# Dummy matmuls in TensorE's idle time, later assumed DMA landings, and expert squares kept in PSUM by VectorE

## The chip, the cores and the metric

One core of a Trainium2 chip runs the whole program. The metric is device time in microseconds, from the start of the launch to its end, lower is better. Engines are named as in the profile: PE is TensorE (PEld its weight loads), DVE is VectorE, ACT is ScalarE, POOL is GpSimd, SP is the engine whose queue issues nearly all DMAs.

## What is computed

Three blocks follow each other: a linear attention with product features, an expert block (two matrix products with a squared ReLU between them and a sigmoid gate), and a gated block that mixes along the sequence with a 1088 x 1088 matrix.

```python
# attention, per batch b and head h (4 x 4, 1088 positions, head width 32, r = 8)
phi(x) = outer(S1 x, S2 x)                    # 64 features
out = phi(q) (phi(k)^T v) / (phi(q) . sum phi(k) + 1e-6)
# expert block, x is (4, 1088, 128)
xk, xr = mu_k*x + (1-mu_k)*x_prev, mu_r*x + (1-mu_r)*x_prev
k = max(xk @ w_k, 0)                          # 128 -> 1024
x = sigmoid(xr @ w_r) * (k*k @ w_v)           # 1024 -> 128
# gated block
h = max(x @ w_in, 0); u, v = halves of h      # 128 -> 2 x 512
v = layernorm(v) over its 512 columns
v_s = w_spatial @ v + b_spatial               # along the 1088 positions
out = (u * v_s) @ w_out                       # 512 -> 128
```

## The kernel before

Everything is kept transposed, features on the 128 partitions and positions along the free axis, and a batch is cut into three chunks of 384, 384 and 320 positions (`CH`). A product that needs full accuracy is made of three passes (`mm3`): each operand is split into a high part H and a low part L of type fp32r, and L·H, H·H and H·L are added up in one PSUM bank.

**Start (0 to 30 us of the trace).** SP loads k, q, v and the expert weights. The weights come as 64-bit numbers and are taken apart by DVE, ACT and POOL (`split64`, L399 to L419). Meanwhile PE makes the attention features of batch 0 (L468, small 64 x 64 products), sums k features over positions (`k_sum`), turns q features (L549) and so on; DVE spreads features into products (L497) and masks the sums (L527). Two groups of matmuls on a zero tile do no work for the result: seven at L1135 and three at L1200, both 384 columns wide into PSUM bank 7.

**Expert loop (30 to about 170 us).** There are 96 units g: 4 batches x 3 chunks x 8 slices of 128 hidden columns. `up(g)` is an `mm3` into one of the PSUM banks 0, 1 and 2, taken in turn, and a ReLU by ACT (L655). `sqsplit(g)` squares and splits. `down(g)` adds the unit's part into bank 3. In the written order a unit's down stands four units behind its up (`LAG`). The letter that `kind(g)` takes from `PAT` says how the square is made:

- P: ACT writes r = ReLU; POOL makes r·r in SBUF (L658); ACT makes H by a second activation (Square, L687); DVE makes L = square - H from SBUF (L395). The bank is free after the ReLU.
- Q: DVE multiplies the bank by r into SBUF (L663); ACT copies that to H; POOL subtracts to L (L395). The bank is free after DVE's multiplication.
- D: ACT squares r once (L675); the down product then runs in plain fp32 (L699, two passes on PE). The bank is free after the ReLU.

Before, `PAT` gives Q to the 13 even units below 26 and P to the 30 even units from 26 to 84 and to 86, 88, 90, 92 and 94; the odd units are D, but for 87, 89, 91 and 93, which are Q.

**Spatial part (from about 150 us).** The w_spatial tiles are loaded into the two small tiles `st`, converted to H and L (`wconv`), and used by `spatial` for batch 0, then by `group` for batches 1 to 3, where sums of quadrants (`sums`, DVE at L914, from raw tiles that `wraw` loads at L911) save products.

**What sets the order.** The program is written in one order, and `arrange` at the end makes another of it: it plays all instructions through with assumed costs (`cost`), gives every engine the ready instruction of lowest rank (written place), assumes when each DMA lands, and then fixes the order on each engine, SP's queue included. So a changed instruction or a changed assumption moves others.

Of the kernel before, what the change touches and what calls it, by code (L numbers as in the profile page):

```python
# [30 lines left out]
VS = (34, 40, 43, 49, 55, 60, 63, 66, 69)  # L31
VN = (72, 85)
CONVP = (512,)
NWARM = 7
NFILL = 3
NFILL2 = 3
VP = 2 * (HD + 1)
G1 = 26
WS = 30
# [14 lines left out]
EP = 2  # L54
G2 = (86, 94)
V2 = 3
PAT = ('QD', 'PD', 'PQ', 'PD')
UT = 'x0'
GLB = 8
GW = 4  # L60
# [29 lines left out]
START = 700  # L90
LEAD = 130
MODE = {64: 93, 128: 100}
SLACK = {"PE": 60, "Activation": 150, "DVE": 150, "Pool": 200, "SP": 0}
RATES = ((3500, 200), (6400, 125), (float("inf"), 352))

# [130 lines left out]
    return type(i).__name__ == "InstDMACopy"  # L226


def arrange(tc, after, chain):

# [31 lines left out]
    for k in reversed(range(len(todo))):  # L264
        if k in follow:
            rank[k] = min(rank[k], rank[follow[k]])

    def release(k):
        e = eng[k]
# [8 lines left out]
    while left:  # L278
        pick = None
        for e in ENGINES:  # L280
            if e == "PE" and forced is not None:
                if forced not in open_[e]:
                    continue
                c = (max(free[e], ready[forced]), forced)
            else:
                if e not in best:
                    first = min((max(free[e], ready[k]) for k in open_[e]), default=None)
                    best[e] = None if first is None else min(
                        (rank[k], k, max(free[e], ready[k])) for k in open_[e] if ready[k] <= first + SLACK[e])
                if best[e] is None:  # L290
                    continue
                c = best[e][2], best[e][1]
            if pick is None or c < pick:
                pick = c
        s, k = pick
        e, i = eng[k], todo[k]
        if is_dma(i):
            if len(lanes) >= 8:
                s = max(s, done[lanes[-8]] + LATENCY[e])
            lanes.append(k)  # L300
            free[e] = s + (473 if e == "SP" else 430)
            t, size = max(s + 1080, wire), 4 * free_size(aps(i.outs)[0]) * aps(i.outs)[0].ap[0][1]
            for until, rate in RATES:
                if t < until:
                    x = min(size, (until - t) * rate)
                    t, size = t + x / rate, size - x
                    if size <= 0:
                        break
            wire = t
            done[k] = t + 450  # L310
        else:
            if e == "PE":
                if i.tile_size[1] != mode:
                    mode = i.tile_size[1]
                    s = max(s, free[e]) + MODE[mode]
                forced = follow.get(k)
            step, end, lock = spent[k]
            if lock:
                lo, hi = port["Pool" if e == "DVE" else "DVE"]
                x = hi - s - LEAD if lo <= s + LEAD < hi else 0  # L320
                step, end = step + x, end + x
                port[e] = s + LEAD + x, s + end
            free[e] = s + step
            done[k] = s + end + 10
        issued[k] = s
        order[e].append(k)
        open_[e].discard(k)
        best.pop(e, None)
        left -= 1
        for k2 in then[k]:  # L330
            missing[k2] -= 1
            if not missing[k2]:
                release(k2)
                best.pop(eng[k2], None)
# [8 lines left out]
def attn_moe_gmlp(ctx: ExitStack, tc: tile.TileContext, qT, kT, va, st, wk, wv, wr, win, wout,  # L343
# [122 lines left out]
    def tiled(out_ap, l, r, start, stop):  # L466
# [4 lines left out]
        if open_visit[0]:  # L471
            visit_last[0] = ins
        return ins

    def visit(*steps):
        open_visit[0], visit_last[0] = True, None
# [170 lines left out]
    def up(g):  # L647
# [8 lines left out]
        if kind(g) == "P":  # L656
            sq = sb(rot(*R), [128, n])
            anchor[2] = GE.tensor_tensor(out=sq, in0=r, in1=r, op=ALU.mult)  # L658
            sqs[g] = (r, sq)
        elif kind(g) == "D":  # L660
            sqs[g] = (r, None)
        else:
            anchor[0] = VE.tensor_tensor(out=r, in0=hk, in1=r, op=ALU.mult)  # L663
            sqs[g] = (None, r)

    def kind(g):
        p = PAT[(g >= G1) + sum(g >= x for x in G2)]
# [460 lines left out]
    winH, winL = sb("winH", [128, DFF], F32R), sb("winL", [128, DFF], F32R)  # L1128
    woH, woL = sb("woH", [128, DG], F32R), sb("woL", [128, DG], F32R)
    T2s = [sb(f"T2{d}", [128, 128], F32R) for d in range(ND)]  # L1130
    zero = sb("mx", [128, CMAX], F32R)
    VE.memset(zero.bitcast(F32), 0.0)
    wp = bank(7)[:, :CMAX]
    for n in range(NWARM):
        TE.matmul(wp, lhsT=zero[:, :128], rhs=zero, start=n == 0, stop=n == NWARM - 1)  # L1135
    VE.memset(ebias, -896.0 * 2 ** 23)
    VE.memset(half, -0.5)
    SE.activation(out=warm, in_=half, func=AF.Sigmoid)
# [49 lines left out]
    def behind(anchors, fn, *a):  # L1188
        fn(*a)

    def warm_up():
        wm = bank(7)[:, :CMAX]
        for n in range(NFILL2):
            TE.matmul(wm, lhsT=wkH[:, :128], rhs=wkH[:, :CMAX], start=n == 0, stop=n == NFILL2 - 1)

    now(q_feat(0, bank(4)[:, :192]))
    q_last = outer[0]
    wq = bank(7)[:, :CMAX]
    for n in range(NFILL):
        TE.matmul(wq, lhsT=zero[:, :128], rhs=zero, start=n == 0, stop=n == NFILL - 1)  # L1200
    kv0 = bank(5)
    k_sum(0, range(2), kv0, range(3))
    q_turn(0)
    k_sum(0, range(2), kv0, range(3, NT))
    k_blocks(0, kv0)
    k_mask0 = list(k_mask)
# [192 lines left out]
                    v_tile(b + 1, NK, (3, 7))  # L1399
    while gout:  # L1400
        gout.pop(0)()
    arrange(tc, after, chain)


_INS = ["qT", "kT", "va", "st", "wk", "wv", "wr", "win", "wout", "wT", "wtail", "btail", "mu", "ident", "msk"]
# [53 lines left out]
```

## Time and profile before

| | us |
|---|---|
| three runs | 446.53, 446.63, 447.45 (median 446.63) |
| profiled execution, its own time | 448.08 |
| its span from first to last instruction | 446.3 |

| engine | busy us | share |
|---|---|---|
| PE | 431.2 | 97% |
| PEld | 401.5 | 90% |
| DVE | 306.4 | 69% |
| ACT | 268.9 | 60% |
| POOL | 230.0 | 52% |

The profiled execution took 448.08 us, of which the profile's span is 446.3; the rest lies before its first and behind its last instruction. Matmul ends are modelled, so PE counts as busy even where its next matmul waits a little; the idle time of PEld and the rows of waits tell more. The mean over the span hides three stages: DVE, ACT and PE are all nearly full in the expert loop, while from 252 us on PE alone is.

### The profile page before, as it was taken

How to read it: one execution, taken by the hardware profiler on the slowest of the kernel's cores; microseconds unless marked ns; L12 is line 12 of the kernel's file. 1: busy time of each engine (PE TensorE's matmuls, PEld its weight loads, DVE VectorE, ACT ScalarE, POOL GpSimd, SP SyncE). 2: the span in 40 equal slices, each digit the busy share in tenths (PEclk: the TensorE clock that was granted, in tenths of full speed). 3: DMA queues.
4: the chain of work that ended last, by engine and by line, in shares of the span. 5: the costliest groups of instructions: out<-in, count | busy, mean ns of one | idle time of the engine just before them, and what ended most of it. 6: DMA issues, size and time to landing. Idle time of an engine off the chain costs nothing.

```text
span 446.3 us, 8451 instructions
## 1 busy us (share of the span) xinstructions
PE 431.2 (97%) x3117; PEld 401.5 (90%) x3117; DVE 306.4 (69%) x531; ACT 268.9 (60%) x629; POOL 230.0 (52%) x271
## 2 busy tenths in 40 slices
PE   8699989999999999999999899999999999999996
PEld 6587879888888889989999799999999999999996
DVE  4879989889998866576557986951847932634414
ACT  2568999989998998664344745444534434434231
POOL 2137688877886779740222646544436626334220
PEclk9569999999999999999999999999999999999999
DMA  7964020011101101421247213232022232100001
GB/s 218 365 230 146 1 56 15 20 37 47 53 20 54 35 20 36 138 61 59 104 150 217 65 61 115 84 94 64 24 84 90 78 95 62 50 10 25 2 0 50
DMA packets 31241, 34.97 MB, mean 78 GB/s; under 512 B 2848, under 2 KB 26848, under 8 KB 31200
## 3 DMA queue, kind: packets, MB, share of 16 engines
q1 hardware_dynamic: 30912, 34.36, 24.2%
q8 instruction: 24, 0.39, 0.3%
q14 instruction: 17, 0.14, 0.1%
q10 hardware_dynamic: 288, 0.08, 0.1%
HBM read 25.91 MB, written 8.52 MB: 77 GB/s over the span
## 4 chain that ended last, share of the span: by engine, by line
PE 75%; DVE 8%; ACT 6%; DMA 5%; POOL 2%; issue 1%; SPq 1%; POOLq 0%; ACTq 0%; DVEq 0%
PE p L389 61%; PE p L468 5%; PE p L699 4%; DMA m<-in_wT_dram 2%; DMA st<-in_wT_dram 2%; DMA w<-in_wk_dram 1%; ACT m L655 1%; PE p L1015 1%; PE p L1014 1%; DVE VR L797 1%; ACT w L392 1%; PE p L549 1%; DVE m L914 1%; DVE m L395 1%; ACT w L675 1%
## 5 line engine op out<-in xcount | busy, mean ns | idle before, releaser
L389 PE MATMUL p<-m,k 128*128 128x384 f32 (+1 forms) x288 | 72.4, 366 | 1.4 <-DVE m L663 1.3
L389 PE MATMUL p<-w,k 128*128 128x384 f32 (+1 forms) x360 | 63.5, 324 | 0.0
L389 PEld LDWEIGHTS p<-w,k 128*128 128x128 f32 x360 | 58.8, 188 | 0.9 <-DVE m L914 0.3
L389 PEld LDWEIGHTS p<-m,k 128*128 128x128 f32 x288 | 50.9, 194 | 9.1 <-DVE m L663 1.8
L914 DVE TENSOR_TENSOR m<-p,m 128x384 f32<-128x384 f32 (+2 forms) x37 | 19.2, 520 | 56.9 <-PE p L1015 56.4
L392 ACT ACTIVATE m<-m 128x384 fp32r<-128x384 f32 (+2 forms) x49 | 24.7, 504 | 44.6 <-DVE m L1028 35.7
L395 POOL TENSOR_TENSOR k<-VR,k 128x512 fp32r<-128x512 f32 x25 | 32.8, 1311 | 30.6 <-ACT k L392 26.1
L655 ACT ACTIVATE m<-p 128x384 f32<-128x384 f32 (+1 forms) x96 | 44.2, 470 | 7.0 <-PE p L389 5.2
L395 DVE TENSOR_TENSOR m<-m,m 128x384 fp32r<-128x384 f32 (+1 forms) x48 | 34.7, 726 | 12.3 <-ACT m L392 9.2
L389 PE MATMUL p<-w,n1H 128*128 128x384 f32 (+1 forms) x192 | 37.2, 325 | 1.0 <-DVE x L863 1.0
L658 POOL TENSOR_TENSOR m<-m 128x384 f32<-128x384 f32 (+1 forms) x35 | 30.9, 886 | 12.1 <-ACT m L655 11.8
L793 POOL TENSOR_SCALAR rs<-mv 128x1 f32<-128x1 f32 x34 | 9.6, 281 | 53.4 <-DVE mv L792 52.3
L392 ACT ACTIVATE m<-p 128x384 f32<-128x384 f32 (+1 forms) x36 | 17.2, 483 | 32.0 <-PE p L389 24.2
L699 PE MATMUL p<-w,wvT 128*128 128x384 f32 (+1 forms) x86 | 33.5, 471 | 0.0
L389 PEld LDWEIGHTS p<-w,n1H 128*128 128x128 f32 x192 | 31.9, 188 | 1.5 <-DVE x L863 1.3
L389 PE MATMUL p<-w,n1L 128*128 128x384 f32 (+1 forms) x168 | 33.1, 323 | 0.0
L395 DVE TENSOR_TENSOR w<-m,w 128x384 fp32r<-128x384 f32 (+1 forms) x35 | 27.4, 785 | 5.9 <-ACT w L687 3.2
L392 ACT ACTIVATE k<-VR 128x512 fp32r<-128x512 f32 x25 | 15.7, 629 | 23.6 <-PE p L389 16.5
L395 POOL TENSOR_TENSOR n1H<-VR,n1H 128x512 fp32r<-128x512 f32 x12 | 16.1, 1343 | 26.0 <-ACT n1H L392 21.9
L389 PEld LDWEIGHTS p<-w,n1L 128*128 128x128 f32 x168 | 28.3, 188 | 0.2
L797 DVE TENSOR_SCALAR VR<-VR,mv,rs 128x512 f32<-128x512 f32 x24 | 20.4, 851 | 10.1 <-POOL rs L794 9.8
L395 POOL TENSOR_TENSOR n1L<-VR,n1L 128x512 fp32r<-128x512 f32 x12 | 15.8, 1316 | 18.7 <-ACT n1L L392 18.5
(286 smaller groups left out, 1178.8 us busy)
## 6 DMA issues: line engine op xcount, KB each, us to landing
vd<-VR SPq DMA_DIRECT2D x24, 256.0 KB, 2.0
VR<-vd SPq DMA_DIRECT2D x24, 256.0 KB, 2.9
st<-in_wT_dram SPq DMA_DIRECT2D x16, 192.0 KB, 2.3
w<-in_kT_dram SPq DMA_DIRECT2D x8, 192.0 KB, 5.0
w<-in_qT_dram SPq DMA_DIRECT2D x8, 192.0 KB, 4.4
VR<-in_wT_dram SPq DMA_DIRECT2D x8, 192.0 KB, 3.0
out_dram<-m SPq DMA_DIRECT2D x8, 192.0 KB, 1.9
m<-in_wT_dram SPq DMA_DIRECT2D x8, 192.0 KB, 3.8
```

Source lines behind the costliest of these rows:

```text
L389: TE.matmul(out_ap, lhsT=l, rhs=r, start=first and n == 0, stop=last and n == 2, skip_group_check=skip)
L392: return SE.activation(out=dst, in_=src, func=AF.Copy)
L395: return eng.tensor_tensor(out=L, in0=src, in1=H.bitcast(F32), op=ALU.subtract)
L468: ins = TE.matmul(out_ap, lhsT=l, rhs=r, start=start, stop=stop)
L549: TE.transpose(pt[:, cut(c, t)], qp[:, t, 128 * g:128 * g + 128], idn)
L655: SE.activation(out=r, in_=hk, func=AF.Relu)
L658: anchor[2] = GE.tensor_tensor(out=sq, in0=r, in1=r, op=ALU.mult)
L675: anchor[1] = SE.activation(out=sq, in_=sqs.pop(g)[0], func=AF.Square)
L699: TE.matmul(vvs[i], lhsT=wvT[:, f // 2], rhs=hls.pop(g), start=f == 0, stop=f == NF - 1)
L793: GE.tensor_scalar(out=rs, in0=mv[:, 1:2], scalar1=1e-6, scalar2=None, op0=ALU.add)
L797: VE.tensor_scalar(out=v, in0=r, scalar1=mv[:, 0:1], scalar2=rs, op0=ALU.subtract, op1=ALU.mult)
L914: return eng.tensor_tensor(out=o, in0=a, in1=b_, op=op)
```

## The change

The dummies: the first group becomes ten matmuls of 256 columns, the second group and an unused helper go. `keep_busy(n)` issues n dummies of 256 columns into bank 7 as one accumulation group and notes their names; it is called with 26 behind the first group and with 45 behind the turn of q's first chunk. `arrange` adds the length of the program to the rank of a noted instruction, so that PE takes it only where nothing else is ready. The zero tile moves to tag `x3`. Since `bank(7)` is used again by `q_turn`, all 26 must be done before that turn, and all 45 before the next one.

Landings: in `arrange`, a DMA that starts later than 30000 ns of the played time is taken to land 1500 ns later than before. Nothing waits longer by itself; only the order may differ.

Squares: the even units get the new letter S. DVE multiplies the bank by r into the bank itself, ACT copies H from the bank, and DVE subtracts bank - H to L. POOL has no part in it. The bank is free only when that subtraction is done. 48 units become S: the 13 that were Q, and the 35 that were P.

```diff
-NWARM = 7
-NFILL = 3
-NFILL2 = 3
+NWARM = 10
+IW = 256
...
-PAT = ('QD', 'PD', 'PQ', 'PD')
+PAT = ('SD', 'SD', 'SQ', 'SD')
...
+MARGIN = (30000, 1500)
+IDLE = (26, 45)
...
-def arrange(tc, after, chain):
+def arrange(tc, after, chain, idle):
...
+    for k, i in enumerate(todo):
+        if i.name in idle:
+            rank[k] += len(todo)
...
-            done[k] = t + 450
+            done[k] = t + 450 + (MARGIN[1] if s > MARGIN[0] else 0)
...
+    idle = set()
+
+    def keep_busy(n):
+        w = bank(7)[:, :IW]
+        for x in range(n):
+            idle.add(TE.matmul(w, lhsT=zero[:, :128], rhs=zero, start=x == 0, stop=x == n - 1).ins.name)
...
-            anchor[0] = VE.tensor_tensor(out=r, in0=hk, in1=r, op=ALU.mult)
-            sqs[g] = (None, r)
+            sq = hk if kind(g) == "S" else r
+            anchor[0] = VE.tensor_tensor(out=sq, in0=hk, in1=r, op=ALU.mult)
+            sqs[g] = (None, sq)
...
-    zero = sb("mx", [128, CMAX], F32R)
+    zero = sb("x3", [128, IW], F32R)
     VE.memset(zero.bitcast(F32), 0.0)
-    wp = bank(7)[:, :CMAX]
+    wp = bank(7)[:, :IW]
     for n in range(NWARM):
         TE.matmul(wp, lhsT=zero[:, :128], rhs=zero, start=n == 0, stop=n == NWARM - 1)
+    keep_busy(IDLE[0])
...
-    wq = bank(7)[:, :CMAX]
-    for n in range(NFILL):
-        TE.matmul(wq, lhsT=zero[:, :128], rhs=zero, start=n == 0, stop=n == NFILL - 1)
     kv0 = bank(5)
     k_sum(0, range(2), kv0, range(3))
     q_turn(0)
+    keep_busy(IDLE[1])
     k_sum(0, range(2), kv0, range(3, NT))
```

Three places where the order changes follow. The first is PE at about 11 to 25 us, from the last k sums of batch 0 to those of batch 1 (`p_81` and `p_82` are the sums of batch 1, `p_72` to `p_78` and `p_73` to `p_79` the features that they need, `x_25` the zero tile). Before:

```order
L468 MATMUL p_54_206<-va_34_138,n1H_181 64x33 x4
L468 MATMUL p_58_255<-kb_57_253,VR_63 64x66 x12
L468 MATMUL p_90_409<-Sbd_117,w_32_132 64x64 x6
L587 MATMUL p_61_274<-idn_64,VR_63 128x128 x3
L468 MATMUL p_72_313<-Sbd_117,w_37_148 64x64 x6
L468 MATMUL p_75_324<-Sbd_117,w_37_148 64x64 x6
L468 MATMUL p_78_335<-Sbd_117,w_37_148 64x64 x6
L468 MATMUL p_81_346<-xs0L_154,w_73_314 64x33 x6
```

And now:

```order
L474 MATMUL p_54_232<-va_35_168,n1H_211 64x33 x4
L486 MATMUL p_57_255<-x_25_92 128x256 x3
L474 MATMUL p_59_327<-kb_58_325,VR_63 64x66 x12
L486 MATMUL p_57_255<-x_25_92 128x256
L474 MATMUL p_91_481<-Sbd_147,w_33_162 64x64 x6
L486 MATMUL p_57_255<-x_25_92 128x256 x4
L600 MATMUL p_62_346<-idn_64,VR_63 128x128 x3
L474 MATMUL p_73_385<-Sbd_147,w_38_178 64x64 x6
L474 MATMUL p_76_396<-Sbd_147,w_38_178 64x64 x6
L474 MATMUL p_79_407<-Sbd_147,w_38_178 64x64 x6
L486 MATMUL p_57_255<-x_25_92 128x256 x31
L474 MATMUL p_82_418<-xs0L_184,w_74_386 64x33 x6
```

Of the 45 dummies, 8 now stand around the first attention products and 31 directly ahead of batch 1's sums. The other six stand behind the third and fourth up; of the 26, all stand ahead of the k features of batch 0, 15, 10 and 1.

The second is DVE behind the mask of batch 1's sums (`kb`), where the first units come (`p_89` in the rows of the change is unit 0's bank). Before:

```order
L527 TENSOR_TENSOR kb_82_383<-p_81_346,mk_65 128x132
L407 TENSOR_SCALAR w_84_389<-w_84_389 128x512
L663 TENSOR_TENSOR m_89_406<-p_88_402,m_89_406 128x384
L497 TENSOR_TENSOR n1L_410<-p_90_409,bs_92_417 128x768
L402 TENSOR_SCALAR w_98_440<-w_68_298 128x512
L404 TENSOR_SCALAR w_99_441<-w_68_298 128x512
```

And now:

```order
L540 TENSOR_TENSOR kb_83_455<-p_82_418,mk_65 128x132
L413 TENSOR_SCALAR w_85_461<-w_85_461 128x512
L677 TENSOR_TENSOR p_89_474<-p_89_474,m_90_478 128x384
L510 TENSOR_TENSOR n1L_482<-p_91_481,bs_93_489 128x768
L401 TENSOR_TENSOR w_96_498<-p_89_474,w_96_498 128x384
L408 TENSOR_SCALAR w_99_512<-w_69_370 128x512
```

The multiplication writes the bank, and the subtraction, which was POOL's, stands in DVE's row one instruction later.

The third is DVE at about 245 us, between the sums of raw w_spatial tiles and the splits of gated products (`m_862` before, `m_828` now, which PE's next output product reads). Before:

```order
L395 TENSOR_TENSOR n0L_3484<-m_855_3411,n0L_3484 128x384
L914 TENSOR_TENSOR VR_63<-VR_63 128x384
L863 TENSOR_TENSOR m_853_3402<-p_854_3404,m_853_3402 128x320
L914 TENSOR_TENSOR VR_63<-m_855_3411,VR_63 128x384
L395 TENSOR_TENSOR m_862_3461<-m_853_3402,m_861_3460 128x320
```

And now:

```order
L877 TENSOR_TENSOR m_819_3439<-p_820_3441,m_819_3439 128x320
L928 TENSOR_TENSOR m_821_3448<-m_821_3448,VR_63 128x384
L401 TENSOR_TENSOR m_828_3498<-m_819_3439,m_827_3497 128x320
L401 TENSOR_TENSOR n0L_3521<-m_821_3448,n0L_3521 128x384
L928 TENSOR_TENSOR VR_63<-VR_63 128x384
L928 TENSOR_TENSOR VR_63<-m_821_3448,VR_63 128x384
```

The product and its split have moved ahead of three instructions of the sums.

## Rows read from the trace of the kernel before

**Rows 1.** Stages: stretch, its length, busy us (instructions) by engine, PEclk, DMA share, GB/s.

```profile
13.00:30.00 17.00, 13.71 (x155) 12.07 (x152) 13.56 (x27) 8.71 (x20) 3.29 (x3) 0.50 0.88 306
30.00:165.00 135.00, 132.99 (x1211) 114.43 (x1210) 121.82 (x202) 125.28 (x317) 102.92 (x108) 1.00 0.16 47
...
240.00:252.00 12.00, 9.99 (x65) 9.21 (x64) 11.54 (x20) 10.16 (x26) 5.36 (x5) 1.00 0.38 115
252.00:446.30 194.30, 190.61 (x1126) 186.18 (x1124) 107.14 (x185) 80.89 (x165) 80.89 (x89) 1.00 0.18 58
```

**Rows 2.** Narrow stretches where the granted clock changes, the same columns.

```profile
12.00:13.00 1.00, 0.40 (x11) 0.43 (x13) 1.00 (x4) 0.68 (x1) 0.00 (x0) 0.92 1.05 388
...
29.50:30.00 0.50, 0.50 (x3) 0.50 (x3) 0.50 (x2) 0.50 (x3) 0.50 (x1) 0.59 1.01 410
```

**Rows 3.** Timeline of the start: start, us, instruction, [idle before <-what ended it].

```profile
1.30 2.10 PEld L1135 LDWEIGHTS p<-mx 128*128 128x128 f32 x7 [1.30 <-DVE half L1137]
...
5.23 1.61 PE L468 MATMUL p<-Sbd,w 128*64 128x64 f32 x36
...
11.49 0.43 DVE L402 TENSOR_SCALAR w<-w 128x512 int32<-128x512 int32 x1 [1.47 <-DMA w<-in_wk_dram]
...
20.93 0.85 PE L468 MATMUL p<-xs0L,w 128*64 128x33 f32 x12 [2.72 <-DVE w L497]
...
25.04 1.90 PE L468 MATMUL p<-xs0L,w 128*64 128x33 f32 x32
...
27.21 0.30 DVE L527 TENSOR_TENSOR kb<-p,mk 128x132 f32<-128x132 f32 x1 [2.30 <-PE p L468]
```

**Rows 4.** The chain that ended last: start, us, what (merged).

```profile
109.74 3.30 PE p L468 x108
...
213.56 6.66 PE p L389 x36
```

**Rows 5.** PEld, 30 to 165 us: group, count, busy us, mean ns, idle before.

```profile
L389 PEld LDWEIGHTS p<-m,k 128*128 128x128 f32 x245 | 42.0, 188 | 8.4 <-DVE m L663 1.8 <-ACT mx L628 0.5 <-ACT m L644 0.2
```

**Rows 6.** DVE, 30 to 165 us, the same columns: subtractions, others, multiplications from PSUM (L663).

```profile
L395 DVE TENSOR_TENSOR w<-m,w 128x384 fp32r<-128x384 f32 x21 | 17.4, 831 | 3.0 <-ACT w L687 2.2 <-ACT w L675 0.7
L629 DVE SCALAR_TENSOR_TENSOR mx<-x,mus,mx 128x384 f32<-128x384 f32 x8 | 7.4, 924 | 1.9 <-ACT mx L628 1.9
...
L395 DVE TENSOR_TENSOR w<-m,w 128x320 fp32r<-128x320 f32 x8 | 5.8, 731 | 0.8 <-POOL m L658 0.6
...
L404 DVE TENSOR_SCALAR w<-w 128x512 int32<-128x512 int32 x4 | 4.6, 1152 | 0.0
...
L663 DVE TENSOR_TENSOR m<-p,m 128x384 f32<-128x384 f32 x8 | 4.3, 549 | 0.4 <-ACT m L655 0.4
...
L395 DVE TENSOR_TENSOR m<-mx,m 128x384 fp32r<-128x384 f32 x7 | 4.0, 577 | 0.1
```

**Rows 7.** Shortest, median and longest ns: L404 (to 30 us) and L629.

```profile
L404 DVE TENSOR_SCALAR w<-w x4: 418/421/1233, 11.8 to 29.5; 128x512 int32<-128x512 int32 x4
...
L629 DVE SCALAR_TENSOR_TENSOR mx<-x,mus,mx x12: 540/672/1460, 40.3 to 164.7; 128x384 f32<-128x384 f32 x8, 128x320 f32<-128x320 f32 x4
```

**Rows 8.** POOL, 30 to 165 us: all squares of L658 (busy, count), then unit subtractions.

```profile
30.00:165.00 135.00, 26.39 (x29) 1.00 0.16 47
...
L395 POOL TENSOR_TENSOR w<-m,w 128x384 fp32r<-128x384 f32 x9 | 9.9, 1103 | 2.7 <-ACT w L392 2.6
...
L395 POOL TENSOR_TENSOR w<-m,w 128x320 fp32r<-128x320 f32 x4 | 4.3, 1074 | 0.8 <-ACT w L392 0.8
```

**Rows 9.** ACT's ReLUs (L655), 30 to 165 us: busy and count.

```profile
30.00:165.00 135.00, 37.86 (x83) 1.00 0.16 47
```

**Rows 10.** Timeline at 247 us: DVE's split and PE's wait for it.

```profile
247.84 1.56 DVE L395 TENSOR_TENSOR m<-m,m 128x320 fp32r<-128x320 f32 x1
...
249.45 0.41 PE L389 MATMUL p<-m,woH 128*128 128x320 f32 x1 [1.59 <-DVE m L395]
```

More of the change, by code (lines that the diff above doesn't have):

```diff
@@ L1189, in behind @@
         fn(*a)
[L1191 to L1194, printed above, removed]
     now(q_feat(0, bank(4)[:, :192]))
     q_last = outer[0]
-    wq = bank(7)[:, :CMAX]
-    for n in range(NFILL):
-        TE.matmul(wq, lhsT=zero[:, :128], rhs=zero, start=n == 0, stop=n == NFILL - 1)
     kv0 = bank(5)
@@ L1401, in attn_moe_gmlp @@
         gout.pop(0)()
-    arrange(tc, after, chain)
+    arrange(tc, after, chain, idle)
 _INS = ["qT", "kT", "va", "st", "wk", "wv", "wr", "win", "wout", "wT", "wtail", "btail", "mu", "ident", "msk"]
```

## The prediction

> **What bounds the kernel now.** I read the stages first. [...] From 30 to 165 us, the expert loop, three engines are nearly full at once: of 135 us DVE is busy for 121.8, ACT for 125.3 and PE for 133.0 [rows 1]. From 252 us to the end PE is busy for 190.6 of 194.3 us and DVE for 107.1 [rows 1]: there PE alone counts, and what is won or lost ahead of it stays in the total.
>
> PE's 133.0 needs a second view, because its ends are modelled. The weight loads of the up products, the largest group in the loop, stood idle for only 8.4 us before them, and no named releaser has more than 1.8 of it [rows 5]. So PE truly works through most of the loop, and relief for the other engines can give back at most about 8 us there, while PE has no slack to hide a delay.
>
> The clock fell inside the stretch from 12 to 13 us (0.92 of it granted) and came back inside the one from 29.5 to 30 (0.59) [rows 2]. Before it fell, PE made small 64-wide attention products and transposes and waited between them; before it rose, it had worked without a gap on full-width up products. In the slow stretch it had two waits to read: PE stood idle for 2.72 us until DVE had the features of batch 1, and DVE for 2.30 us until PE had summed them (the mask `kb`) [rows 3]. The first is the hole that the dummies are to fill, the second is a price of the slow clock on the engine that is nearly full afterwards.
>
> **Term A, the start.** The pace at either clock comes from rows. A 64-wide pass takes 1.90/32 = 59 ns in the slow stretch [rows 3] and 3.30/108 = 31 ns later [rows 4]. A 384-column pass takes 6.66/36 = 185 ns later [rows 4], and the seven first dummies took 2.10/7 = 300 ns per weight load, the slow pace [rows 3]. A 256-column dummy I put at two thirds of these: 0.20 us slow, 0.12 fast, an estimate.
>
> Ahead of batch 0's features now stand 10 + 15 dummies: 25 x 0.20 = 5.0 us from 1.30, so 6.3, and some 0.4 more for the change of groups, where the first product started at 5.23 before [rows 3]. That is 1.5 us late, and the 11 dummies between the features add 1.3 at the fast pace, of which the faster products give back a part. DVE had 1.47 us of idle time ahead of the first weight conversion at 11.49, which waits for its DMA [rows 3], and that hides it. Without that cover the cost is up to 1.5 us on DVE; I take 0, because the landing sets 11.49 either way.
>
> The 31 dummies stand in the hole of 2.72 us. At the fast pace they take 31 x 0.12 = 3.7 us; but the 36 features passes ahead of them shrink by 36 x (59 - 31) = 1.0 us, so they fit (2.7 + 1.0). Behind them come 72 passes of k sums and four passes of the first ups: at the fast pace 72 x 0.031 + 4 x 0.185 = 3.0 us, where the slow clock needed until 27.2 from 20.9. DVE then has its features at about the same time as before, and the mask need not wait: the 2.30 us go. What is late next is DVE's own queue, which is as full after 30 us as before. So A = -2.3. Ends: if PE's lead also shortens DVE's work around it, -4; if the clock falls all the same, the 31 dummies take 31 x 0.20 = 6.2 us in a hole of 2.7, and PE is 3.5 us late, +3.5 less what follows at a better clock.
>
> **Term B, the loop.** 42 of the 48 S units lie in the window: 29 squares of POOL (26.4 us) and 13 subtractions (9.9 + 4.3) are gone from it, 40.6 of POOL's 102.9 us, 39% [rows 1, 8]. DVE gains one instruction per unit: for the former P the multiplication from the bank, for the former Q the subtraction. The nearest row is the multiplication at L663, which reads the bank and SBUF: 549 ns [rows 6]. Writing into a bank and reading H beside a bank has no row for DVE; I take 0.55, with ends of 0.48 and 0.65, since the only difference is the side that is written. 42 x 0.55 = +23.1 us.
>
> Against that, DVE waits less. Its subtractions from SBUF took 831 and 731 ns on average [rows 6], 29 of them; from the bank at 549 they save 21 x 0.28 + 8 x 0.18 = 7.3 us. These long times are time lost to POOL: L404 takes 421 ns before POOL has work and 1152 in the loop, L629 540 at best and 924 on average [rows 6, 7], together 4 x 0.73 + 8 x 0.38 = 6.0 us. Over the 14 groups of that kind in the same view, of which these two are shown, the same difference adds up to 25 us, an estimate. With 39% of POOL's work gone I take 39% of that away: 9.7 us (ends 0 and 16).
>
> Sum for DVE: 121.8 + 23.1 - 7.3 - 9.7 = 127.9 of 135, 95%. ACT reads H from the bank instead of SBUF, which changes nothing that the sum would show. So DVE is fuller, but not over the edge, and PE keeps the lead: B = 0. Ends: -4, half of the 8.4 us of idle weight loads, and +8 (first rival).
>
> [...] The multiplication that reads the bank takes 549 ns and a subtraction of the same 384 columns from SBUF alone 577 on average [rows 6]: no surcharge for PSUM shows. [...] The row decides, and I stay with 0.55.
>
> **Term C, the later landings.** PE stood still at 249.45 for 1.59 us, until DVE had split a gated product; that split itself took 1.56 us at 247.84 [rows 10]. From 240 to 252 us PE was busy for 9.99 of 12 [rows 1]. In the new order the product and its split stand ahead of three instructions of the sums that ran before it, so I expect some 1 us of the 2.0 back; what is late next is the sums themselves, which PE reads later. C = -1.0, ends -2.0 and +1.5, the latter if a sum that was pushed back becomes the wait. Of the DMA queue, only the places of six loads against each other change, with one instruction between them.
>
> **The sum.** -2.3 + 0 - 1.0 = -3.3. Against the profiled execution, 448.08, that is 444.8. It lies 1.45 above the median of the runs, 446.63, so against the median I get **443.3**. A difference of 0.2%, 0.9 us, is about what a measurement of this kernel can tell from no change.
>
> **Rivals.**
>
> *The bank becomes the wait (slower).* A ReLU comes every 135/83 = 1.63 us [rows 9], so with three banks in turn a bank has 4.9 us from one up to the next. An S unit holds it for three passes, 0.56, a ReLU (37.9/83 = 0.46 [rows 9]), DVE 0.55, a copy like the ReLU 0.46, and DVE 0.55: 2.6. Four queue waits must fit into the other 2.3 us. For it: ACT and DVE are 93% and 95% full, and one instruction of 0.55 ahead in each makes 2.2. Against it: the played order knows of the banks and has moved ups apart. If each S unit comes 0.2 us late, 42 x 0.2 = +8.4: 443.3 + 8.4 = 451.7. It turns the sign from about 0.08 us per unit on, where it has eaten A and C.
>
> *The clock falls anyway (no change).* Between about 7 and 17 us only eight dummies stand among the small products and transposes, not many more than the nothing that stood there when the clock fell [rows 2]. Then the dummies ahead of batch 1's sums run slowly: +3.5, and the work from 20.9 to 27.2, then at a clock that has come back under them, gives 6.3 x 0.47 = 2.9 back: A = +0.6, and 446.63 + 0.6 - 1.0 = 446.2. For it: the order has few dummies there. Against it: three of them close the wait ahead of the first attention product.
>
> *The loop gains too (faster).* With POOL at 62 of 135 us its links in the chain go, and half the idle time of the weight loads, 4.2 us [rows 5], comes back: 443.3 - 4.2 = 439.1. For it: POOL's subtractions ended waits of PE before. Against it: DVE takes over that very work.
>
> **How the numbers follow.** I give the forecast 0.45 (its own range 440.5 to 446), the bank 0.25, the clock 0.12 and the gain in the loop 0.18. The range goes from 438, a little below the last rival, to 451, where the milder half of the first one lies; about 0.17 is left outside. Faster by over 0.2% (below 445.7): nearly all of forecast and third rival and a little of the second, 0.62. Within 0.2%: most of the second and the edges of forecast and first, 0.13. Slower: the rest of the first, 0.25.
>
> **What would show it.** A is right if the granted clock is 1.00 from 13 to 30 us, the wait of DVE's mask is gone and the first ReLU comes before 23; wrong if PE works on dummies when batch 1's features are ready. B is right if DVE is busy for about 128 us in as long a loop, L404 and L629 come nearer to their shortest times, and PE's up loads idle no longer than 8.4 us; a bank as the wait shows as up loads that wait for DVE's subtraction. C is right if PE is busy for over 10.5 of the 12 us around the same product. The prediction is wrong as a whole if the loop lasts over 3 us longer.

## The result and the profile after

The changed kernel takes **441.92 us** (median of 4 runs, 441.45 to 442.16), the kernel before 446.58 (4 runs, 445.24 to 447.45): a ratio of 0.989, 95% interval 0.9869 to 0.991. The forecast was 443.3 (438 to 451). The profiled execution took 442.08 us, its span is 440.3.

The stages of the changed kernel, with the columns of [rows 1]:

```profile
13.00:30.00 17.00, 16.96 (x236) 15.04 (x234) 15.56 (x31) 11.61 (x26) 3.35 (x4) 1.00 0.95 317
30.00:165.00 135.00, 134.77 (x1217) 115.67 (x1217) 119.68 (x245) 127.56 (x324) 61.30 (x69) 1.00 0.15 45
165.00:200.00 35.00, 35.00 (x202) 33.71 (x201) 22.63 (x44) 22.69 (x57) 17.36 (x20) 1.00 0.29 86
240.00:252.00 12.00, 11.14 (x73) 10.67 (x72) 11.86 (x18) 9.06 (x23) 6.24 (x6) 1.00 0.18 56
252.00:440.30 188.30, 184.34 (x1087) 180.37 (x1086) 102.57 (x176) 77.61 (x158) 79.02 (x86) 1.00 0.18 58
```

Of the signs that the forecast named, some are there: the clock is 1.00 from 13 to 30 us, the wait of DVE's mask is gone, L642 (L629 before) takes 732 ns instead of 924, and PE is busy for 11.14 of the 12 us around the late gated product. Others are not: the first ReLU comes at 24.34 us and not before 23, DVE is busy for 119.68 us in the loop and not for about 128, and the up loads idle for 9.7 us and not for at most 8.4 (all below). POOL is down from 102.92 to 61.30 us in the loop. The stretch from 252 us to the end, 188.3 against 194.3 us [rows 1], shows the whole lead over that one execution of before.

The start, on PE's weight loads, DVE and ACT (one view per engine, merged in order of time):

```profile
3.73 3.16 PEld L486 LDWEIGHTS p<-x 128*128 128x128 f32 x15 [0.35 <-PE p L1149]
7.03 0.43 PEld L474 LDWEIGHTS p<-Sbd,w 128*64 128x64 f32 x12
...
18.46 3.77 PEld L486 LDWEIGHTS p<-x 128*128 128x128 f32 x31
...
12.40 0.42 DVE L408 TENSOR_SCALAR w<-w 128x512 int32<-128x512 int32 x1
...
26.08 0.29 DVE L540 TENSOR_TENSOR kb<-p,mk 128x132 f32<-128x132 f32 x1
...
24.34 0.49 ACT L668 ACTIVATE m<-p 128x384 f32<-128x384 f32 x1 [1.07 <-PE p L395]
```

The mask `kb` of batch 1 no longer waits, as forecast. But the features start at 7.03 us where they started at 5.23 [rows 3], the first weight conversion comes at 12.40 instead of 11.49 and does not wait for its DMA any more, and the first ReLU comes at 24.34, not before 23.

DVE in the loop (30 to 165 us; columns as in [rows 6]), and what PE's weight loads waited for from 30 to 260 us (total, times, longest):

```profile
L677 DVE TENSOR_TENSOR p<-p,m 128x384 f32<-128x384 f32 x31 | 17.3, 558 | 3.2 <-ACT m L668 2.8
L401 DVE TENSOR_TENSOR w<-p,w 128x384 fp32r<-128x384 f32 x30 | 16.4, 550 | 4.0 <-ACT w L398 3.9
L642 DVE SCALAR_TENSOR_TENSOR mx<-x,mus,mx 128x384 f32<-128x384 f32 x8 | 5.9, 732 | 0.6 <-ACT mx L641 0.6
L625 DVE SCALAR_TENSOR_TENSOR mx<-mx,mus,x 128x384 f32<-128x384 f32 x7 | 4.3, 613 | 0.5 <-POOL mx L624 0.4
L411 DVE SCALAR_TENSOR_TENSOR w<-w,w 128x512 int32<-128x512 int32 x4 | 3.4, 847 | 0.0
L401 DVE TENSOR_TENSOR w<-st,w 128x384 fp32r<-128x384 f32 x6 | 3.2, 548 | 0.0
```

```profile
PEld p L395 <- DVE w L401: 2.7, 11, 0.5
PEld p L395 <- ACT m L398: 1.5, 2, 1.1
```

The loads of the up products from 30 to 165 us (as [rows 5]):

```profile
L395 PEld LDWEIGHTS p<-m,k 128*128 128x128 f32 x249 | 42.1, 189 | 9.7 <-DVE w L401 2.5 <-ACT m L657 0.4 <-ACT m L668 0.4
```

Multiplying into a bank takes 558 ns and subtracting from one 550: the 0.55 that the forecast took. No up waits longer than 0.5 us for DVE's subtraction. But these short waits are 2.7 us in all, 2.5 of them ahead of up loads in the loop: the sign that the forecast named for the bank is there, at a third of the 8.4 us of its rival.

### The profile page after: what moved, and what is told of

Same layout as the page of the kernel before. It is cut to its first block, busy times and chain, and to the rows that moved or that the text cites. A ratio compares the mean times of both kernels' runs of the same rounds, so it can differ in the third digit from the quotient of the medians.

```text
span 440.3 us, 8526 instructions
## 1 busy us (share of the span) xinstructions
PE 433.7 (98%) x3188; PEld 404.9 (92%) x3188; DVE 303.7 (69%) x579; ACT 269.0 (61%) x629; POOL 179.0 (41%) x223
## 4 chain that ended last, share of the span: by engine, by line
PE 90%; DVE 7%; ACT 2%; POOL 1%; issue 0%; POOLq 0%; ACTq 0%; DVEq 0%
PE p L395 70%; PE p L713 6%; PE p L474 5%; PE p L486 2%; PE p L562 2%; PE p L1029 1%; PE p L1028 1%; DVE VR L811 1%; PE p L600 1%; DVE n1L L510 1%; DVE bn L805 1%; PE p L1149 1%; DVE m L928 1%; DVE VR L928 0%; PE p L876 0%; PE p L875 0%
## 5 line engine op out<-in xcount | busy, mean ns | idle before, releaser
L395 PEld LDWEIGHTS p<-m,k 128*128 128x128 f32 x288 | 48.3, 189 | 10.4 <-DVE w L401 2.7
L668 ACT ACTIVATE m<-p 128x384 f32<-128x384 f32 (+1 forms) x96 | 44.8, 472 | 3.1 <-PE p L395 2.7
L401 POOL TENSOR_TENSOR k<-VR,k 128x512 fp32r<-128x512 f32 x25 | 32.6, 1303 | 32.7 <-ACT k L398 28.3
L398 ACT ACTIVATE m<-p 128x384 f32<-128x384 f32 (+2 forms) x40 | 19.0, 479 | 31.7 <-PE p L395 23.6
L401 DVE TENSOR_TENSOR m<-m,m 128x384 fp32r<-128x384 f32 (+1 forms) x44 | 29.7, 678 | 9.5 <-ACT m L398 8.9
L807 POOL TENSOR_SCALAR rs<-mv 128x1 f32<-128x1 f32 x34 | 8.5, 249 | 57.2 <-DVE mv L806 56.8
L677 DVE TENSOR_TENSOR p<-p,m 128x384 f32<-128x384 f32 (+1 forms) x48 | 25.7, 535 | 5.0 <-ACT m L668 4.6
L401 DVE TENSOR_TENSOR w<-p,w 128x384 fp32r<-128x384 f32 (+1 forms) x44 | 23.3, 532 | 4.8 <-ACT w L398 4.6
L401 POOL TENSOR_TENSOR n1H<-VR,n1H 128x512 fp32r<-128x512 f32 x12 | 16.2, 1349 | 24.5 <-ACT n1H L398 19.8
L805 DVE BATCH_NORM_STATS2 bn<-VR 128x6 f32<-128x512 f32 x24 | 16.5, 688 | 11.4 <-ACT VR L801 11.2
```

The costliest lines, as they stand in the source:

```text
L395: TE.matmul(out_ap, lhsT=l, rhs=r, start=first and n == 0, stop=last and n == 2, skip_group_check=skip)
L398: return SE.activation(out=dst, in_=src, func=AF.Copy)
L401: return eng.tensor_tensor(out=L, in0=src, in1=H.bitcast(F32), op=ALU.subtract)
L668: SE.activation(out=r, in_=hk, func=AF.Relu)
L677: anchor[0] = VE.tensor_tensor(out=sq, in0=hk, in1=r, op=ALU.mult)
L805: VE.bn_stats(out=bn, in_=r)
```

## The experiments

Each run below stands against the kernel before on the same chip (446.2 to 446.6 us in the median).

**One part alone.** The first: the changed kernel, its letters and landings as before.

```diff
-PAT = ('SD', 'SD', 'SQ', 'SD')
+PAT = ('QD', 'PD', 'PQ', 'PD')
-MARGIN = (30000, 1500)
+MARGIN = (30000, 0)
```

> Only the dummies, the old letters and the old landings. Measured by the moment at which PE has done a given amount of work that counts (dummies left out), the changed kernel is 1.5 us ahead of the old one at 28 us, 3.5 at 72, 3.2 at 188, 4.5 at 198 and 6.3 from 250 us on. Theory 'three parts add up': the dummies give the first 1.5 us and perhaps half of what comes until 72, so 1.5 to 2.5 us less than before (about 444.5); clock 1.00 from 13 to 30 us. Rival 'it is all the clock': what comes later is the start's lead handed on, and this kernel alone gives 4.7 us, about 442. Rival 'luck of the order': single parts bring gains and losses that don't add up, and this one may be anywhere within 3 us of before.

Measured: 446.25 against 446.24 us, ratio 1.000 (0.9989 to 1.0012), with the clock at 1.00 throughout. The dummies are worth nothing here by themselves, the steady clock and the later start taken together; both that theory and the rival "it is all the clock" fall. What a steady clock would give without the later start, this run does not show.

The second: the kernel before with the new squares, by the same lines as in the change.

```diff
-PAT = ('QD', 'PD', 'PQ', 'PD')
+PAT = ('SD', 'SD', 'SQ', 'SD')
```

> Only the squares in PSUM, the old dummies and landings. Theory 'three parts add up': the start is as slow as before (clock 0.50 from 13 to 30 us), POOL's load in the loop falls to about 62 us and DVE's does not rise, and the time falls by about 1 to 2 us (445). Rival 'it is all the clock': 446.6. Rival 'the bank holds things up', my forecast's first rival, hidden by the other parts: over 448.

Measured: 445.22 us, 0.9976 (0.9965 to 0.9988); POOL 61.1 us in the loop, DVE 118.6, clock 0.70 on average from 13 to 30. The squares help, by 1.0 us, and of the bank only short waits show (ten, 3.0 us in all).

The third: the kernel before with the later landings.

```diff
-            done[k] = t + 450
+            done[k] = t + 450 + (1500 if s > 30000 else 0)
```

> Only the later landings, on the kernel before. Theory 'three parts add up': the two waits of PE near 190 to 200 and 240 to 250 us get shorter, 1.3 to 3 us less than before (444 to 445), and nothing changes ahead of 150 us but the order. Rival 'luck of the order': these waits go only because all three changes move the instructions there; alone the landings give less than 1 us either way.

Measured: 444.53 us, 0.9960 (0.9947 to 0.9973): 1.7 us, by itself. Not luck that needs the other two, but not all of it need be the landings'. All five executions have a mean clock of 0.990 to 0.992, which of 73 executions of the kernel before only 17 have, with a median of 445.55: against those it is 1.0 us. And in the profile all engines keep the order of before until about 111 us, while the clock comes back some 3 us earlier than in the second profile of before (below), so that PE is 1.5 us ahead at 50 and at 100 us of work (counted as in the next section), before the order differs. With the dummies on both sides, where the clock is steady, the landings give 1.7 us (446.25 and, below, 444.57).

**One part left out** of the changed kernel: in turn the dummies (the second kernel with the landings of the third), the letters, and the landings.

```diff
-            done[k] = t + 450
+            done[k] = t + 450 + (1500 if s > 30000 else 0)
...
-PAT = ('SD', 'SD', 'SQ', 'SD')
+PAT = ('QD', 'PD', 'PQ', 'PD')
...
-MARGIN = (30000, 1500)
+MARGIN = (30000, 0)
```

> Squares in PSUM and later landings, with the old dummies. Alone the dummies gave nothing (446.25 against 446.24), the squares 1.0 us and the landings 1.7, while the whole change gave 4.7. Theory 'the dummies only count once DVE is relieved' (POOL's relief lets the lead at 28 us survive): this kernel is 443.5 or more, so that the dummies are worth 1.5 to 2 us in this company. Rival 'the dummies are worth nothing at all': 442, like the changed kernel. Rival 'the front dummies cost': below 441.5, as features start 1.8 us earlier.

> Dummies and later landings, squares as before. Theory 'the dummies only count once DVE is relieved': 444.5, like the landings alone; POOL is busy for 103 us of the loop again and PE's lead at 28 us is lost by 75. Rival 'each pair has its own luck': anywhere from 442 to 446. If parts simply added up: 444.5 too, so this run speaks for the theory only together with the one without dummies.

> Dummies and squares in PSUM, landings as before. Parts adding up give 445.2 (446.24 - 1.0). Theory 'the dummies only count once DVE is relieved': 443.5 to 444, as far ahead at 150 us of the trace as the changed kernel (3.2 us at 180), and the waits of PE near 195 and 245 us are back (about 3 us).

Measured: 443.03 (0.9918, 0.9896 to 0.994) without dummies, 444.57 (0.9947, 0.9928 to 0.9966) without squares, 445.15 (0.9970, 0.9955 to 0.9984) without landings. Together, as the difference to before:

| kept | us | | kept | us |
|---|---|---|---|---|
| dummies | 0.0 | | squares and landings | -3.4 |
| squares | -1.0 | | dummies and landings | -1.8 |
| landings | -1.7 | | dummies and squares | -1.2 |
| | | | all three | -4.7 |

Squares and landings work alone and somewhat better together. By the medians the dummies add 0.2 us at most to either of the others (the intervals leave up to about 1 us open), and some 1.3 us to both together; since the intervals of 0.9918 and 0.989 overlap, the times do not settle that one, and the traces place 0.8 us of it (next section). The theory that the dummies count as soon as DVE is relieved had 443.5 to 444 for dummies and squares; at 445.15 it falls, and adding up the single parts (445.2) was nearer.

The named waits of PE say why. Of the three rows that cost the kernel before over 1 us each (its second profile, 30 to 260 us),

```profile
PEld p L389 <- DVE m L395: 2.0, 2, 1.8
PEld p L389 <- DVE m L663: 1.8, 2, 1.6
...
PEld p L389 <- DVE x L863: 1.1, 1, 1.1
```

the middle one, an up that waits for DVE's multiplication of a Q unit, stands with 1.8 us in all four profiles with the old letters (the line has another number in two of them) and among the largest waits of none of the four with the new ones. The other two, near 246 and 190 us, stand in all four with the old landings (1.0 to 2.1 and 1.0 to 1.3 us) and among the largest of none with the later ones; the largest wait near 246 us is then one of 1.1 for ACT's H. So squares and landings each take away waits of their own. With the squares, 2.7 to 3.1 us of short waits for DVE's subtraction come in, which speaks for why 1.8 us of wait bring only 1.0.

**Where the operands lie.** The square goes to SBUF, and both parts are read there:

```diff
-            sq = hk if kind(g) == "S" else r
+            sq = r
```

> The changed kernel, but DVE writes the square of an S unit to SBUF, over r, and ACT's copy and DVE's subtraction read it from there; POOL still has no part in it, and the bank is free after the multiplication. Theory 'relief of POOL': what made DVE fast is that POOL has less to do; the subtraction from SBUF takes 0.50 to 0.60 us, close to the 0.56 from the bank, and the time stays within 1 us of the changed kernel. Rival 'reading from PSUM': two operands in SBUF bring the old times of 0.73 to 0.83 us back, 40 x 0.2 = 8 us more of DVE, and the kernel is 2 to 6 us slower. Should the bank have been the wait, it would be 1 to 2 us faster.

Measured: 442.18 us, 0.9911 (0.9897 to 0.9925), against 441.92. DVE in the loop:

```profile
L401 DVE TENSOR_TENSOR w<-m,w 128x384 fp32r<-128x384 f32 x31 | 20.4, 657 | 3.9 <-ACT w L398 3.8
L677 DVE TENSOR_TENSOR m<-p,m 128x384 f32<-128x384 f32 x32 | 17.4, 548 | 0.9 <-ACT m L668 0.7
```

The subtraction takes 657 ns from SBUF, above what the theory said and below the rival, against 550 from the bank; the multiplication 548 against 558. Where the square lies matters to DVE (124.41 us in the loop, against 119.68) and hardly to the time. Neither the bank's being free earlier nor the two SBUF operands decided; that the one gave what the other cost, this run cannot rule out.

**POOL's load put back.** PE's order stays nearly the same, but about a fifth of DVE's instructions stand elsewhere:

```diff
             sq = hk if kind(g) == "S" else r
+            if kind(g) == "S":
+                GE.tensor_tensor(out=sb(rot(*R), [128, n]), in0=r, in1=r, op=ALU.mult)
```

> The changed kernel, with a square by POOL added for each S unit (r times r into a tile that nobody reads), so that POOL has about 48 x 0.9 us more to do while DVE's and PE's orders stay nearly as they are. Theory 'relief of POOL makes DVE fast': DVE's busy time from 30 to 165 us goes from 119.7 back up by 6 us or more, its groups that work from SBUF alone (L410, L411, L642) get slower, those that read a bank (L677, L401 from p) stay at 0.55, and the kernel loses 1 to 3 us. Rival 'the links count, not the load': PE no longer waits for work that passes through POOL, nobody waits for the added squares, and the time stays within 0.5 us of the changed kernel although DVE is slower.

Measured: 448.26 us, 1.0034 (1.0021 to 1.0048): 6.3 us slower than the changed kernel, more than the 1 to 3 expected, and slower than before. DVE is busy for 123.02 us of the loop, 3.3 more than after and not 6. The groups of DVE that answer to those shown after:

```profile
L679 DVE TENSOR_TENSOR p<-p,m 128x384 f32<-128x384 f32 x28 | 15.5, 557 | 0.8 <-ACT m L668 0.6
L401 DVE TENSOR_TENSOR w<-p,w 128x384 fp32r<-128x384 f32 x27 | 14.8, 551 | 1.8 <-ACT w L398 1.7
L642 DVE SCALAR_TENSOR_TENSOR mx<-x,mus,mx 128x384 f32<-128x384 f32 x8 | 6.4, 795 | 0.6 <-ACT mx L641 0.6
L625 DVE SCALAR_TENSOR_TENSOR mx<-mx,mus,x 128x384 f32<-128x384 f32 x7 | 6.0, 852 | 0.0
L411 DVE SCALAR_TENSOR_TENSOR w<-w,w 128x512 int32<-128x512 int32 x4 | 3.9, 979 | 0.1
L401 DVE TENSOR_TENSOR w<-st,w 128x384 fp32r<-128x384 f32 x6 | 3.8, 631 | 0.0
```

What reads a bank stays at 557 and 551 ns; the four groups shown that work from SBUF alone go from 732 to 795, 613 to 852, 847 to 979, 548 to 631. So these got slower with POOL's load back, together with what the other order adds. Not all that works from SBUF alone got slower: L410, which the expectation names, went from 813 to 608, and `w<-x,w` (L401, 128 columns) from 574 to 406. With it POOL is busy for 95.5 us of the loop, nearly as full as before (102.92 [rows 1]); so an S unit whose work is only added to DVE costs: 448.26 is 3.7 us above the run without squares (444.57). By this run the relief of POOL gives 6.3, and the difference of the two is what the squares are worth in this company. How much of the 6.3 us is slow DVE work, how much the other order and how much the longer hold of the tiles r was not separated.

**The kernel before, profiled again.**

> The kernel before, unchanged, profiled once more. Its shown profile was of an execution of 448.08 us in which the clock was 0.50 from 13 us on, and a mean clock of 0.981; most other executions show a mean of 0.987 to 0.992. The kernel with later landings alone has the same order until about 75 us, and there the clock fell at 20 to 22 us only and PE was 2.1 us further by 28 us. Theory 'the shown profile was of an early fall': this profile reads 0.50 from about 20 us on, PE is 1.5 to 2.2 us further by 28 us than in the first profile, and the time is 445.5 to 446.8. Rival 'the early fall is the rule': 0.50 from 13 us on again. In both cases the idle weight load of 1.57 us that waits for DVE's multiplication near 64 us is there.

Measured: 446.29 us, 0.9996 (0.9979 to 1.0014). Three stretches of this profile:

```profile
13.00:30.00 17.00, 12.70 (x147) 11.20 (x145) 14.63 (x28) 9.88 (x21) 4.57 (x4) 0.72 0.94 331
17.00:20.00 3.00, 0.36 (x12) 0.36 (x12) 2.96 (x6) 1.73 (x5) 1.12 (x1) 1.00 1.03 395
20.00:22.00 2.00, 2.00 (x23) 1.46 (x19) 1.99 (x4) 0.93 (x3) 0.14 (x1) 0.58 1.03 359
```

Here PE stood nearly idle from 17 to 20 us at a granted clock of 1.00, and the clock fell right after, at some 20.3 us and not at 12.8. The mean clock of the first profiled execution was 0.981; of the 73 executions of before that were timed beside these runs, four show 0.981 and the others 0.987 to 0.992. So the execution on which the forecast rests had an early fall that is rare. The wait near 64 us is in this profile too, 1.56 us.

**The front dummies.** First without the 26 (`IDLE = (0, 45)`), then also with landings 2500 ns later, then with 8 back:

```diff
-IDLE = (26, 45)
+IDLE = (0, 45)
...
-MARGIN = (30000, 1500)
+MARGIN = (30000, 2500)
...
-IDLE = (0, 45)
+IDLE = (8, 45)
```

> The changed kernel without the 26 dummies of the first group that give way: only the ten at the start stay, and the 45 later ones. The first product of the features comes at about 4.6 us instead of 7.0, the first weight conversion of DVE waits for its DMA again (11.0 to 11.5 instead of 12.4). Theory 'the front dummies cost what they delay': the clock stays at 1.00 thanks to the other 45, and the kernel is 0.5 to 1.5 us faster, 440.5 to 441.4. Rival 'without them the clock falls': the granted clock shows 0.50 from some point between 7 and 22 us on, and the time is 442 to 443.5.

Measured: 441.96 us, 0.9903 (0.9872 to 0.9934), but in two groups: 440.47 to 441.15 and 442.76 to 443.84, with a mean clock of 0.998 or more in all. The clock did not fall; the lower group is where the theory had it, the upper one is not.

> The changed kernel without the 26 dummies of the first group (as in the run without front dummies, whose fastest executions took 440.5 to 441.2 and whose median was 441.96), and landings 2500 ns later instead of 1500. What is left of the wait of PE near 246 us (0.85 us on ACT's H of a gated product, which stood behind an H that waited 1.19 us for a sum) may go. Theory 'later landings act by moving the product ahead of the sums': 0.3 to 1 us faster than the run without front dummies, 441 to 441.6 in the median. Rival 'luck of the order': anything from 440.5 to 444, since the order changes at some hundred places.

Measured: 441.76 us, 0.9891 (0.985 to 0.9932), in two groups 4 us apart. The profile is of an execution of the upper group; PE's weight loads at its start:

```profile
4.42 1.39 PEld L474 LDWEIGHTS p<-Sbd,w 128*64 128x64 f32 x24 [1.03 <-DVE Sbd L1157]
...
14.47 1.40 PEld L474 LDWEIGHTS p<-kb,VR 128*64 128x64 f32 x24 [0.23 <-issue]
...
20.78 3.29 PEld L486 LDWEIGHTS p<-x 128*128 128x128 f32 x27
```

24 passes take 1.39 and 1.40 us, 58 ns each, the pace that the first profile of before had at a granted clock of 0.50 (59 ns [rows 1, 3]), until about 20 us; yet the granted clock reads 1.00 in every stretch. In the profile without front dummies of the lower group the same 24 passes at `kb` took 0.78 us at 13.34. These two profiles suggest that the two groups are two moments, near 11 and near 20 us, at which PE comes to full pace. They are one profile of each group, of two kernels, so it is not shown; and why the pace comes at the one or the other, no row tells.

> The kernel of the last run (no front dummies, landings 2500 ns later) with 8 of the 26 front dummies back, which is the only difference in the order of PE, DVE, ACT and POOL. That kernel's times fell into two groups, 439.3 to 439.8 and 443.7 to 444.0; in the profiled execution of the upper group a 64-wide pass took about 57 ns until 20 us, though the granted clock reads 1.00. In all profiles of kernels that began with 4 us of dummies in a row, passes are fast (32 to 36 ns) from about 7 us on. Theory 'front dummies buy the full pace early, and 8 are enough': features start at 5.4 us, passes are fast before 8 us in the profile, one group of times remains, with a range below 1.5 us and a median of 439.3 to 440.3, the best of this case. Rival 'it is something else, such as when the loads land': two groups again, median between 439.5 and 444.

Measured: **439.60 us** (439.08 to 439.74), 0.9838 (0.9817 to 0.9858), one group. The start and the stage of the late product:

```profile
3.73 1.78 PEld L486 LDWEIGHTS p<-x 128*128 128x128 f32 x8 [0.35 <-PE p L1149]
5.73 2.16 PEld L474 LDWEIGHTS p<-Sbd,w 128*64 128x64 f32 x48 [0.22 <-issue]
7.99 0.81 PEld L474 LDWEIGHTS p<-xs0H,n0H 128*64 128x64 f32 x24
...
10.73 0.43 DVE L408 TENSOR_SCALAR w<-w 128x512 int32<-128x512 int32 x1 [0.21 <-DMA w<-in_wk_dram]
```

```profile
240.00:252.00 12.00, 11.98 (x78) 11.40 (x77) 11.68 (x20) 7.89 (x20) 5.94 (x6) 1.00 0.19 58
```

The features start at 5.73, their delay fits into DVE's wait for its DMA (0.21 us of it is left), and the pace is full by 8 us (24 passes in 0.81). From 240 to 252 us PE has no wait left. This kernel is the best of the case, 2.3 us better than the change. Two edits part them, 8 front dummies for 26 and landings 1000 ns later still; by the table below 1.8 us of the lead are there at 10 us of work, 1.5 at 200, and 0.8 more come between 200 and 220, at the late product.

## Why the prediction came out as it did

The time was right within 1.4 us, and the sum's three terms were each wrong or half right. To place the gain, I took PE's matmuls in order of time, counted each by its columns at the full pace (a plain fp32 pass as nearly two, an estimate: 64 columns more make it 54 ns longer in the trace of before, 486 against 432, and a pass of `mm3` 28, 337 against 309; 405 us in all, dummies left out), and read when each amount was reached; the second profile of before stands against the one after and against the last kernel:

```
work done   before (2nd)   after    diff     last kernel
 10 us         26.16       26.40    +0.2        24.56
 40 us         62.61       61.84    -0.8        60.04
 50 us         74.67       71.78    -2.9        69.97
160 us        190.33      187.75    -2.6       186.26
170 us        201.36      197.74    -3.6       196.26
200 us        231.57      227.96    -3.6       226.48
220 us        253.67      249.00    -4.7       246.68
400 us        435.36      430.67    -4.7       428.29
```

**A, the start (forecast -2.3).** This is the term that failed, at two places. The step "DVE had 1.47 us of idle time ahead of the first weight conversion [...] and that hides it": the conversion came at 12.40, without a wait, 0.9 us later than in the first profile of before and 1.5 later than in the second (10.87). The front dummies ran at the slow pace (15 in 3.16 us, 211 ns each, where the 31 later ones took 122), to 6.9 us where 6.3 was worked out, and the 11 dummies between the features, which I had put at 1.3 us "of which the faster products give back a part", used up the rest of the cover. And the step from rows 2 and 3 took a rare execution for the rule: with the usual fall at 20 us there was less to win. Against that execution A gave 1.5 us by 26 us; against the usual one nothing by then, and 0.0 alone in the time. The dummies did hold the clock (1.00 from 13 to 30 us, where the two profiles of before have 0.50 and 0.72), and the mask's wait did go. In company that gave something later on: counted in the same way, the run without dummies is level with the changed kernel at 10 us of work, and from 40 to 400 it is 0.8 to 0.9 us behind. Near 28 us its six transposes run at a granted clock of 0.50, those of the changed kernel at 1.00 (first the run without dummies):

```profile
28.04 1.40 PEld L549 LDWEIGHTS p<-idn,n1L 128*128 128x128 f32 x6
...
28.09 0.68 PEld L562 LDWEIGHTS p<-idn,n1L 128*128 128x128 f32 x6
```

So, by one profile of each, A was about -0.8 in this company and not -2.3.

**B, the loop (forecast 0).** The price was right: 0.55 per multiplication. The relief was too small: DVE came to 119.68 us, not 127.9. The terms -9.7 (39% of the time lost to POOL) and the 7.3 of the subtractions were mis-sized together by 8.2 us. Part of that is POOL's relief beyond my rule of proportion: L411 (L405 before) went from 1296 to 847 and the subtraction from `st` from 726 to 548 ns, and with POOL's load put back they took 979 and 631. But POOL's load put back brought only 3.3 of DVE's 8.2 us back (in a window that held 239 of its instructions instead of 245); where the rest lies stays open. So B was not 0 but about -2.0: from 10 to 160 us of work the lead goes from +0.2 to -2.6, and 0.8 of these 2.8 us is the dummies'. Two things the forecast had not put together: the relief of POOL is worth more than DVE's sum shows (6.3 us, by the run with POOL loaded, where DVE's sum moved by 3.3), and it pays for the 48 instructions more. In the trace the gain shows at one place, the 1.6 us of PE behind DVE's multiplication near 64 us, which [rows 5] had (1.8) and the forecast passed over. DVE's queue there, and PE's load behind it, in the second profile of before:

```profile
62.19 0.95 DVE L497 TENSOR_TENSOR n1L<-p,bs 128x768 f32<-128x768 f32 x1
64.45 0.97 DVE L629 SCALAR_TENSOR_TENSOR mx<-x,mus,mx 128x384 f32<-128x384 f32 x1 [1.30 <-ACT mx L628]
65.34 0.87 DVE L663 TENSOR_TENSOR m<-p,m 128x320 f32<-128x320 f32 x2
...
65.87 0.44 PEld L389 LDWEIGHTS p<-m,k 128*128 128x128 f32 x3 [1.56 <-DVE m L663]
```

The multiplication stood behind an instruction that waited 1.30 us for ACT, and PE behind the multiplication. In the new order that place is gone, and between 40 and 50 us of work PE gains 2.1 us; the run with POOL loaded has the new letters and not this wait (from 56 to 72 us its longest is 0.4), and loses its time at others. So the wait went with the letters' order, not with POOL's relief.

The reading of [rows 6] that no surcharge for PSUM shows held: the subtraction takes 550 ns from the bank, beside 548 (from `st`) and 657 (the same square) from SBUF.

**C, the later landings (forecast -1.0).** Right in its place and too small. The stage around the product gave 1.1 us (200 to 220 us of work), as forecast; the forecast did not see that the same edit takes the wait near 190 us too, another 1.0 (160 to 170). Alone the landings were worth 1.0 to 1.7, by which executions of before they are held against.

**The rivals.** The bank did not become the wait that the rival feared: at most 0.5 us at a time and 2.7 in all, and the square in SBUF, which frees the bank early, was no faster. The clock did not fall. "The loop gains too" is what happened, at about half its size (-2.0 where it had -4.2), and it does not show where the rival looked: the up loads idled for longer than before, 9.7 against 8.4 us [rows 5].

So the total was near by luck: a start put at 2.3 us that gave about 0.8, and a loop and a stage put at 0 and 1.0 that gave about 2.0 and 2.1, nearly cancelled.

## What to carry to other kernels

Read the clock and the starting pace from more than one execution before you put a price on them: the profile that is shown may be the one run in eighteen. Dummies ahead of the first work are worth what they save in pace less what they delay, so give them no more length than the next engine's wait for its DMA covers (here 8 fitted, with 0.21 us of that wait left, and 26 did not: the conversion came at 12.40 us instead of 10.87). And look for single waits of over 1 us in which an engine's fixed order stands on a stranger's input: three such waits (1.8, 1.6 and 1.1 us), each in a row of its own, were most of what this change took away, and the mean load of no engine showed them.

## What was not expected of the hardware

- PE can work at half pace while the granted clock reads 1.00: 58 ns per 64-wide pass until 20 us in one execution, 32 to 36 ns from 8 us on in those of the changed kernel and of the one with 8 front dummies. The times of that first kernel lie in two groups 4 us apart; that the pace is what parts them is likely and not shown.
- The moment at which the clock falls differs between executions of one kernel: about 12.8 us in the first profile of before, 20.3 in the second. In both PE had stood idle for most of the time just ahead of it (0.40 of 1.00 us busy [rows 2], 0.36 of 3.00), in the first in pieces of under 1 us, in the second for 3.64 of the 5 us from 15 to 20.
- Some 0.9 us of POOL work per S unit, with no reader, cost 6.3 us in all, with the change of order that it brought. Instructions of DVE that read a bank beside one SBUF operand did not feel it (557 and 551 ns); the four groups shown with both operands in SBUF got 9% to 39% slower, and another got faster (574 to 406 ns).
